# Routed attention and a gated feed-forward layer on one core: the first batch in query blocks of 128, 256 and 384, with the feed-forward layer's input and output halves as separate pieces

## The chip, the cores and the metric

The kernel runs on one core of a Trainium2 chip. The metric is the device time of one execution in microseconds (us); lower is better. Most executions of one kernel agree within 1%. A time without further words is a median; a "span" is the time from the first to the last instruction of the profiled execution, some 2 us less than the time.

Five engines work side by side, each with its own instruction queue: PE (TensorE matmuls; PEld is its weight load), ACT (ScalarE), DVE (VectorE), POOL (GpSimd) and SP (here it only issues DMAs).

## The reference, cut to what matters

```python
batch, n_heads, seq, head_dim = (4, 8, 768, 64)     # 16 clusters
q_assign = argmax(q_n . c_n)                        # nearest centroid, per head
k_assign = argmax(k_n . c_n)
mask = q_assign[:, :, :, None] == k_assign[:, :, None, :]
scores = where(mask, scale * q @ k.T, -1e9)
attn = softmax(scores)                              # the sum has + 1e-9 added
x = (attn @ v).transpose(0, 2, 1, 3).reshape(3072, 512)
gate = 1 / (1 + exp(-(x @ w_gate)))                 # 512 -> 1536
val = x @ w_val
return (gate * val) @ w_out                         # 1536 -> 512, float32
```

## The kernel before

For each batch, Q and K are turned so that the head dimension lies on the partitions (the tile `T`). Sixteen more rows hold the one-hot cluster of each query or key, scaled by 2048. A score matmul then contracts 80 rows, and a pair of the same cluster gets a large bonus, which is taken off again as the bias of the exp. That is the whole mask. To build the one-hot rows a batch needs a chain of steps: load, split into a high and a low half (DVE), transpose, logits against the centroids (PE, matmuls of 16 columns), one-hot (DVE), transpose of the one-hot, and a copy of its rows to partitions 64 to 79 of `T`.

A batch is worked off in two blocks of 384 queries. A block has 24 steps (4 pairs of heads times 6 chunks of 128 keys). A step is two score matmuls, one exp and six AV matmuls of 65 columns. The AV matmuls of a step stand one step behind its exp:

```python
    def att(b, qb):
        pend = None
        def av_part(pr, j, es, av):
            ...                                     # six matmuls of 65 columns
            if j == NCH - 1:                        # end of a pair of heads
                s = smp.tile([128, 2, QCH, D + 1], FP, name="avs")
                nc.vector.tensor_tensor(s, av, SV[b], ALU.add)   # operands cut
                ...                                 # 1/sum, then x on POOL
        for pr in range(NPR):
            for j in range(NCH):
                sc = scp.tile([128, 2, 512], FP, name="sc")
                for hh in range(2):
                    nc.tensor.matmul(out=sc[:, hh, 0:QB], ...)   # 80 rows, 384 columns
                es = esp.tile([128, 2, QB], HP, name="es")
                nc.scalar.activation(es, sc[:, :, 0:QB], AF.Exp, bias=nbias, scale=es_scale)
                yield
                if pend is not None:
                    av_part(*pend)
                if j == 0:
                    av = avp.tile([128, 512], FP, name="av")
                pend = (pr, j, es, av)
                yield
        av_part(*pend)
        ...                                         # xT: DMA transpose of x
```

The feed-forward layer (FFN) of a block is one generator of 132 matmuls (96 of 384 columns into `f`, with tanh on ACT, then 36 of 512 columns). It is fed in small portions between the attention steps of the next block. So the first block has no FFN to mix with, and the last block's FFN runs alone at the end.

The preparation of the next batch is laid out by a plan of steps. Its one-hot rows come last, for all heads at once, by a DMA transpose and then eight row DMAs for each side:

```python
    def prep_oh(b, side):
        ohf = OH[b, side].rearrange("p c h x -> p (c h x)")
        nc.vector.tensor_scalar(ohf, ohf, OHV, None, ALU.mult)
        ohT = ohp.tile([128, NCH, 128], HP, name=f"ohT{side}")
        nc.sync.dma_start_transpose(out=ohT, in_=ohf)
        for h in range(H):
            nc.sync.dma_start(out=T[b, side][D : D + NCL, h, :], in_=...)

    # in plan(b): steps of the 48 of the batch before
        if b == 1:
            a_at = (18, 24, 30, 35)                 # splits and DMA transposes, per pair
            b_at = (26, 32, 38, 42)                 # logits and one-hot, per pair
            oh_at = 44
        else:
            a_at, b_at, oh_at = (4, 12, 20, 27), (12, 20, 28, 35), 37
        ...
        at(oh_at, prep_oh, b, 1)
        at(oh_at + 1, prep_oh, b, 0)

    LAG = 5                                         # steps before the FFN of the block before starts
    for b in range(B):
        for qb in range(NQB):
            for half, _ in enumerate(att(b, qb)):
                if half == 2 * LAG and prev is not None:
                    fq.append(ffn(*prev))
                ...                                 # preparation of the plan
                ffn_some(132.0 / (2 * NST + 1))
```

Batch 0 prepares pair 0, and pair 1 but for its one-hot rows, before its first step, and the rest between the steps of its first block. Everything stands in program order on every engine (`tc.manual_schedule()`).

The softmax here doesn't subtract the row's maximum and nothing guards it: scores larger than these inputs give would overflow.

## Time and profile before

| | before |
|---|---|
| time, median of 3 runs (range) | 385.73 us (383.76 to 386.23) |
| span of the profiled run | 381.8 us |
| mean granted TensorE clock | 0.924 |
| first exp / last exp of batch 0 | 21.5 / 100.6 us |
| first FFN matmul | 66.6 us |
| first exp of batches 1, 2, 3 | 111.0, 195.8, 277.8 us |

The page of the profile gives each engine's busy time with its share of the span, and then 40 equal slices of the span (9.5 us each), each with a digit in tenths. PEclk is the clock that TensorE was granted.

```profile
PE 352.7 (92%) x3570; PEld 218.5 (57%) x3570; DVE 161.7 (42%) x319; ACT 234.5 (61%) x322; POOL 59.7 (16%) x62
...
PE   8777897999749979999999799999999999999995
...
PEclk9859655799959989999999989999999999999999
```

PE is the bound, but it is not evenly used: apart from the very last slice, and two slices (15 and 23) in which AV waits 2.3 us for DVE, the low digits of both rows lie in the first twelve slices. The next view sums each engine's busy time in chosen stretches; the columns are named in its first line.

```profile
core 0: us, PE busy (x) PEld busy (x) DVE busy (x) ACT busy (x) POOL busy (x), PEclk, DMA share, GB/s
22.00:40.00 18.00, 14.14 (x192) 10.85 (x193) 10.09 (x18) 9.57 (x11) 4.60 (x3) 0.85 1.15 212
40.00:58.00 18.00, 17.06 (x175) 9.15 (x172) 7.11 (x14) 13.96 (x15) 2.46 (x2) 0.53 0.76 212
58.00:73.00 15.00, 13.39 (x129) 8.03 (x128) 10.77 (x17) 7.54 (x10) 4.19 (x5) 0.54 0.92 177
73.00:100.00 27.00, 26.05 (x359) 18.20 (x357) 15.05 (x34) 17.89 (x27) 2.93 (x3) 1.00 0.38 84
100.00:120.00 20.00, 12.60 (x74) 5.75 (x73) 2.85 (x6) 5.77 (x8) 0.82 (x1) 0.74 0.43 105
```

Between 40 and 58 us PE is "busy" 17.06 of 18.00 us and yet does only 175 matmuls, at a clock of 0.53; between 73 and 100 us it does 359 in 27 us at full clock. Busy time alone hides this. The timeline of the same kernel (start, duration, engine, line, operation, and in brackets the idle time before it and what ended it) shows one step at the low clock:

```profile
52.71 0.83 PE L380 MATMUL sc<-T_184,T_185 80*128 80x384 f16 x2
...
53.45 0.35 PEld L343 LDWEIGHTS <-es 128*128 128x128 f16 x6 [0.60 <-ACT es L388]
53.45 0.51 PE L343 MATMUL av<-va,es 128*128 128x65 f16 x6
53.64 0.90 ACT L388 ACTIVATE es<-sc,nbias 128x768 f16<-128x768 f32 x1 [0.24 <-PE sc L380]
```

PE's weight load waits for the exp and the exp waits for the scores, so neither engine is full.

The chain of waits (the work that ended last, in order of time: start, duration, what) shows a second loss, at the start of batch 1:

```profile
102.12 0.45 PE f L434 x2
...
105.13 2.79 DMA ohT_1649<-oh_422
...
107.94 1.85 DMA T_421<-ohT_1649
...
109.92 0.48 PE sc L380
```

From 102.5 to 109.9 PE waits: first for the SP queue, then for the transpose of the one-hot tile, then for the row DMAs. The list of waits (engine and line, what it waited for, total us, times, longest) sizes that, and the stalls of AV behind the V-mean addition:

```profile
PE sc L380 <- DMA T_421<-ohT_1649: 7.4, 1, 7.4
...
PE av L343 <- DVE avs L353: 5.5, 3, 2.3
```

### The profile page before, as it was taken

Reading aid. Unit: us, or ns where it says so; the run is one execution under the profiler, and the core shown is the slowest. Engines: PE = TensorE matmul, PEld = TensorE weight load, DVE = VectorE, ACT = ScalarE, POOL = GpSimd, SP = SyncE. Lnnn points to the kernel's source line nnn. Section 1 sums busy time; section 2 is a strip of 40 time slices with the busy share of each in tenths; the row PEclk is TensorE's granted clock in tenths of the full one; section 3 lists DMA queues with packets and bytes.
Section 4 is the critical chain, followed back from the end, with each engine's and each line's share of the span. In section 5 each row is a group of like instructions: output and inputs, shape, how many; then the busy total and the mean of one; then the engine's idle time right before and its main releaser. Section 6 shows DMA issues by size and latency. Waiting matters only on the chain.

```text
span 381.8 us, 8564 instructions
## 1 busy us (share of the span) xinstructions
PE 352.7 (92%) x3570; PEld 218.5 (57%) x3570; DVE 161.7 (42%) x319; ACT 234.5 (61%) x322; POOL 59.7 (16%) x62
## 2 busy tenths in 40 slices
PE   8777897999749979999999799999999999999995
PEld 3655644667415646566656566566656655665552
DVE  5765628475303456635315637534303421331330
ACT  3347676566416747576767565676768877884331
POOL 5943103200100000320000000220000010100000
PEclk9859655799959989999999989999999999999999
DMA  7999788940129682780239674941230004002202
GB/s 246 297 215 209 220 195 134 277 98 10 39 54 267 183 198 72 127 228 19 45 73 267 167 219 85 193 102 30 49 103 29 0 3 124 1 2 47 79 2 82
DMA packets 76071, 45.72 MB, mean 120 GB/s; under 512 B 57152, under 2 KB 71936, under 8 KB 76032
## 3 DMA queue, kind: packets, MB, share of 16 engines
q1 hardware_dynamic: 73280, 40.42, 42.6%
q0 software_dynamic: 2608, 4.72, 6.7%
q8 instruction: 28, 0.46, 0.5%
q14 instruction: 11, 0.09, 0.1%
q10 hardware_dynamic: 144, 0.03, 0.0%
HBM read 28.34 MB, written 6.29 MB: 91 GB/s over the span
## 4 chain that ended last, share of the span: by engine, by line
PE 80%; DMA 5%; issue 4%; POOL 3%; DVE 3%; ACT 2%; SPq 1%; ACTq 0%; POOLq 0%; DVEq 0%
PE f L416 33%; PE f L434 17%; PE sc L380 16%; PE av L343 9%; PE f L186 3%; DMA nat<-in_q_dram 2%; POOL hl L173 2%; DMA xT<-x 2%; PE f L317 1%; ACT es L388 1%; DVE hl L174 1%; DMA ohT_1649<-oh_422 1%; SPq L76 1%; DVE avs L353 1%; DVE hl L173 1%
## 5 line engine op out<-in xcount | busy, mean ns | idle before, releaser
L388 ACT ACTIVATE es<-sc,nbias 128x768 f16<-128x768 f32 x192 | 172.6, 901 | 92.5 <-PE sc L380 89.5
L427 DVE SCALAR_TENSOR_TENSOR hT<-g,f 128x384 f16<-128x384 f32 x96 | 53.0, 553 | 119.8 <-PE f L416 81.8
L416 PE MATMUL f<-xT,wg 128*128 128x384 f16 x384 | 99.0, 333 | 1.2 <-DMA xT<-x 1.2
L416 PE MATMUL f<-xT,wv 128*128 128x384 f16 x384 | 93.2, 329 | 0.5 <-ACT g L425 0.5
L343 PEld LDWEIGHTS <-es 128*128 128x128 f16 x1152 | 63.0, 102 | 43.2 <-issue 9.4
L434 PE MATMUL f<-wo,hT 128*128 128x512 f16 x288 | 78.0, 388 | 0.0
L343 PE MATMUL av<-va,es 128*128 128x65 f16 x1152 | 70.9, 200 | 6.7 <-DVE avs L353 5.5
L365 POOL TENSOR_TENSOR x<-avs,ri 128x384 f16<-128x384 f32 x32 | 27.9, 873 | 285.6 <-DVE ri L364 214.1
L425 ACT ACTIVATE g<-f 128x384 f32<-128x384 f32 x96 | 46.8, 487 | 23.5 <-PE f L416 13.8
L416 PEld LDWEIGHTS <-wg 128*128 128x128 f16 x384 | 34.5, 99 | 19.5 <-issue 3.6
L416 PEld LDWEIGHTS <-wv 128*128 128x128 f16 x384 | 33.5, 98 | 16.3 <-issue 1.5
L434 PEld LDWEIGHTS <-hT 128*128 128x128 f16 x288 | 25.7, 99 | 21.6 <-issue 2.3
L174 DVE SCALAR_TENSOR_TENSOR hl<-nat,hl 128x768 f16<-128x768 f32 x32 | 33.5, 1046 | 3.0 <-POOL hl L173 2.1
L380 PE MATMUL sc<-T_184,T_185 80*128 80x384 f16 x96 | 31.4, 420 | 0.5
L380 PE MATMUL sc<-T_421,T_423 80*128 80x384 f16 x96 | 24.7, 337 | 7.4 <-DMA T_421<-ohT_1649 7.4
L173 DVE TENSOR_SCALAR hl<-nat 128x768 f16<-128x768 f32 x26 | 18.1, 696 | 22.1 <-DMA nat<-in_k_dram 22.0
L353 DVE TENSOR_TENSOR avs<-av,sv 128x390 f32<-128x390 f32 x32 | 17.9, 559 | 20.6 <-PE av L343 20.5
L380 PE MATMUL sc<-T_1731,T_1733 80*128 80x384 f16 x96 | 23.9, 330 | 0.0
L197 DVE TENSOR_REDUCE mx<-f 128x12 f32<-128x192 f32 x32 | 11.3, 354 | 28.9 <-PE f L186 28.9
L380 PE MATMUL sc<-T_3046,T_3048 80*128 80x384 f16 x96 | 23.5, 325 | 0.0
L443 ACT ACTIVATE osb<-f 128x512 f32<-128x512 f32 x24 | 14.3, 594 | 13.5 <-PE f L434 12.9
L380 PEld LDWEIGHTS <-T_423 80*128 80x128 f16 x96 | 9.6, 101 | 15.9 <-issue 9.1
(82 smaller groups left out, 199.7 us busy)
## 6 DMA issues: line engine op xcount, KB each, us to landing
nat<-in_k_dram SPq DMA_DIRECT2D x16, 384.0 KB, 5.4
nat<-in_q_dram SPq DMA_DIRECT2D x16, 384.0 KB, 6.0
vn<-in_v_dram SPq DMA_DIRECT2D x8, 768.0 KB, 5.6
out_dram<-osb SPq DMA_DIRECT2D x24, 256.0 KB, 2.7
wg<-in_moe_w_gate_dram POOLq DMA_DIRECT2D x1, 1536.0 KB, 12.3
wv<-in_moe_w_val_dram POOLq DMA_DIRECT2D x1, 1536.0 KB, 19.7
wo<-in_moe_w_out_dram POOLq DMA_DIRECT2D x1, 1536.0 KB, 27.0
T_423<-ohT_1618 SPq DMA_DIRECT2D x8, 24.0 KB, 1.9
```

Source lines behind the costliest of these rows:

```text
L173: (eng or nc.vector).tensor_scalar(hl[:, :, 0, :], nat, SC, None, ALU.mult)
L174: nc.vector.scalar_tensor_tensor(hl[:, :, 1, :], nat, SC, hl[:, :, 0, :], ALU.mult, ALU.subtract)
L343: nc.tensor.matmul(out=av[:, o : o + D + 1], lhsT=es[:, hh, bass.ts(t, 128)], rhs=VA[b][:, 2 * pr + hh, j, :], start=(j == 0 and hh == 0 a ...
L353: nc.vector.tensor_tensor(s, av[:, 0 : 2 * QCH * (D + 1)].rearrange("p (h t d) -> p h t d", h=2, t=QCH), SV[b][:, 2 * pr : 2 * pr + 2, :] ...
L365: nc.gpsimd.tensor_tensor(x[:, :, 2 * pr * D : 2 * (pr + 1) * D].rearrange("p t (h d) -> p h t d", h=2), s[:, :, :, 0:D], ri.unsqueeze(3). ...
L380: nc.tensor.matmul(out=sc[:, hh, 0:QB], lhsT=T[b, 1][0 : D + NCL, h, bass.ts(j, 128)], rhs=T[b, 0][0 : D + NCL, h, bass.ts(qb, QB)], start ...
L388: nc.scalar.activation(es, sc[:, :, 0:QB], AF.Exp, bias=nbias, scale=es_scale)
L416: nc.tensor.matmul(out=gv[i][:, 0:QB], lhsT=w[:, dc, bass.ts(fc, 128)], rhs=xT[:, :, dc, :], start=(dc == 0), stop=(dc == NDC - 1),)
L425: nc.scalar.activation(g, gv[0][:, 0:QB], AF.Tanh, scale=0.5)
L427: nc.vector.scalar_tensor_tensor(hT[:, fc, :], g, 1.0, gv[1][:, 0:QB], ALU.add, ALU.mult)
L434: nc.tensor.matmul(out=o, lhsT=hT[:, fc, bass.ts(t, 128)], rhs=wo[:, fc, :], start=(fc == 0), stop=(fc == NFC - 1),)
L443: nc.scalar.activation(osb, o, AF.Copy, scale=0.5)
```

## The change

The intent is to start sooner and to have FFN work to mix in sooner:

- **Batch 0 in three blocks.** The first has 128 queries. It needs every key of the batch but only a sixth of the queries (`qn0`, loaded first), and has eight exps, each over three key chunks. The second has 256 queries and takes the first one's FFN input half. The third has 384 queries and takes the first one's output half and the whole FFN of the second.
- **FFN as two generators**, `ffn_in` and `ffn_out`; the first block's output half is held back (`held`) to the third block. The weights come in ten pieces instead of three.
- **AV stands two steps behind the exp** in blocks of 256 and 384 queries.
- **One-hot rows per pair of heads**, turned by PE transposes (`rows`), in place of one DMA transpose for all heads; the splits of a pair are issued half a step apart.
- **V sums on POOL** (`sum_v`), so in batches 1 to 3 a mean takes one matmul where six stood.
- **Order by a model.** In the first block and up to the middle of the third, the compiler's scheduler is free to reorder PE, ACT and DVE by its own model of times. It keeps program order only on SP and POOL.
- **Smaller parts.** In batch 0, half of each split of K runs on ACT where most stood on POOL (2.17 us each). The first two pairs of batch 1, and `x` of the first two blocks, are transposed by PE. In the kernel before, a DMA transposed `x`, and its first transpose took 6.14 us, up to the first FFN matmul. In batches 1 to 3 the FFN starts 7 steps into a block instead of 5.

The core of the diff, with cuts marked by "...":

```diff
-    ctx.enter_context(tc.manual_schedule())
+    first = ExitStack()
+    first.enter_context(tc.manual_schedule())
...
-    load_pair(0, 0)
-    load_pair(0, 1)
+    qn0 = natp.tile([128, H, D], FP, name="nat")
+    nc.sync.dma_start(out=qn0, in_=...)             # 128 queries of every head
+    for pr in range(NPR):
+        load_side(0, pr, 1)                         # all keys
     load_v(0, 0)
-    load_pair(0, 2)
-    load_pair(0, 3)
     load_v(0, 1)
+    for pr in range(NPR):
+        load_side(0, pr, 0)                         # queries last
...
-    def prep_oh(b, side):
-        ...                                         # DMA transpose, 8 row DMAs
+    def rows(b, pr):
+        ns = 1 if b == 0 else 2
+        po = fp_.tile([32 * ns, 1024], HP, name="f")
+        for c in range(NCH):
+            nc.tensor.transpose(po[:, bass.ts(c, 128)], ..., ident)
+        ohc = ohp.tile([32 * ns, S], HP, name="ohc")
+        nc.vector.tensor_scalar(ohc, po[:, 0:S], OHV, None, ALU.mult)
+        for side in range(ns - 1, -1, -1):
+            for hh in range(2):
+                nc.sync.dma_start(out=T[b, pr, side][D : D + NCL, hh, :], in_=...)
...
+    def sum_v(b, g):
+        ...                                         # three additions on POOL
...
-    def att(b, qb):
+    def att(b, c0, n):
+        pend = []
+        G = 3 if n == 1 else 1                      # key chunks per exp
...
-                if pend is not None:
-                    av_part(*pend)
+                if len(pend) == (1 if G > 1 else 2):
+                    av_part(*pend.pop(0))
+                pend.append((pr, j0, es))
...
-    def ffn(b, qb):
+    def ffn_in(b, c0, n):
+    ...
+    def ffn_out(b, c0, n):
...
+    BLK = [[(0, 1), (1, 2), (3, 3)]] + [[(0, 3), (3, 3)]] * (B - 1)
...
+    def by_dma(b, pr, load, a, base):
+        at(base, load, load_pair, b, pr)
+        for i, side in enumerate((1, 0)):
+            at(base, a + 0.5 * i, split, b, pr, side)
+            at(base, a + 0.5 * i, trans_dma, b, pr, side)
+            at(base, a + 9 + i, classify, b, pr, side)
+        at(base, a + 11.5, rows, b, pr)
...
+    def first_block():
+        ...
+        first.close()
+        first.enter_context(
+            tc.manual_schedule(engines={mybir.EngineType.SP, mybir.EngineType.Pool})
+        )
+        ...
+            if pr == 2:
+                prep_v(0, 3, nc.scalar)             # the V cast of the last pair, on ACT
...
+                lag = 14 if b > 0 else {1: 7, 3: 9}[c0]
+                pieces = {(0, 1): 110, (0, 3): 132}.get((b, c0), 132)
+                for half, _ in enumerate(att(b, c0, n)):
+                    if (b, c0, half) == (0, 3, 24):
+                        first.close()
+                        ctx.enter_context(tc.manual_schedule())
+                    if half == lag:
+                        fq.append(ffn_in(*prev))
+                        if (b, c0) == (0, 1):
+                            held.append(ffn_out(*prev))
+                        else:
+                            fq += held
+                            held = []
+                            fq.append(ffn_out(*prev))
```

## The prediction

> **What bounds the kernel now.** TensorE, once fed. The busy table gives PE 352.7 of 381.8 us. In the timeline from 123 us, one attention step (two score, six AV, 5.5 FFN matmuls) takes 1.4 to 1.5 us without a gap: 0.33 + 0.18 + 5.5 x 0.1625. A full-clock block of 384 queries with an FFN block is then about 35.5 us of PE, the whole kernel about 323 (estimate: 8 blocks, 32 logit groups at 0.75, V sums, batch-0 transposes). The other 59 us are lost, about 44 of them before 110 us:
> - The first exp starts at 21.5 us (timeline).
> - From 38 to 73 us the granted clock is 0.5 to 0.57 (windows): block 0 has no FFN, ACT and PE wait for each other, the first FFN matmul waits for xT until 66.6. The Trainium skill, "TensorE: Matmul & The Clock Gate", Part 1, says half rate is the default and returns after an idle window; this trace agrees (0.50 in 50 to 60 us).
> - From 102.5 to 109.9 PE waits for batch 1's one-hot rows (chain of waits: issue queue, DMA transpose, row DMAs), then runs at half clock to about 116.
> - At 134.2 and about 216 AV waits 2.3 us for the V-mean addition, which stands behind two splits in VectorE's queue.
>
> **What the change does.**
> 1. Block of 128 queries first: first exp at about 13.5 us, 8 earlier. Eight exps (0.90) suffice, but it carries all K preparation, 20 to 23 us each of ACT and DVE work: it ends at 33 to 38.
> 2. 256 queries with FFN input for the first 128: PE about 18.5 us at full clock, ACT about 20; ends at 54 to 60. FFN starts near 38, not 66.6.
> 3. 384 queries with 96 FFN-in matmuls of 256 columns (0.108), 36 FFN-out (0.216) and batch 1's preparation: about 40 us of PE; batch 1 starts at 95 to 98, not 110.
> 4. Batch 1's rows come per pair: the 7.4 us stall goes (part of the 95), plus about 3 us at half clock.
> 5. Later batches: AV lags two steps and splits are issued apart, so the 2.3 us stalls and clock dips mostly go (3 to 5). V sums lose 10 of 12 matmuls of 0.115 per batch (3.4).
> 6. Added on PE: transposes for two pairs of batch 1 (3.4), row transposes (4.7 over three batches, 2.6 more in batch 0), short FFN matmuls (1.2): about 12 us.
>
> **Sum.** Batch 1 starts 13 us earlier (steps 1 to 4 less their added work), 3 of clock, 7 from step 5, minus 3 of row transposes after batch 0: 20 us. Span about 360, time **363 us**, range **354 to 375**. Chances: faster 0.87, same 0.09, slower 0.04.
>
> **What would show it.** First exp before 15 us; first FFN matmul before 42; first scores of batch 1 before 100 with no wait over 2 us on row DMAs; clock above 0.8 on average in 40 to 100; batches 2 and 3 about 80 us apart, not 82; the tail (last FFN block) unchanged.
>
> **What would make it wrong.** The 128-query block is a long chain over four in-order engines: if it ends after 42, the gain halves. The clock may stay at half in the 256-query block. Weights load in ten pieces behind V: a late quarter stalls FFN. The first stage is ordered by a scheduler's model, perhaps badly.

## The result, and the profile after

| | before | after |
|---|---|---|
| time, median (range) | 385.06 us (383.76 to 386.23, 4 runs) | 365.42 us (364.88 to 366.35) |
| span | 381.8 | 363.4 |
| mean granted clock | 0.924 | 0.993 |
| first / last exp of batch 0 | 21.5 / 100.6 | 17.2 / 89.4 |
| first FFN matmul | 66.6 | 37.5 |
| first exp of batch 1 | 111.0 | 92.5 |
| first exp of batch 2 | 195.8 | 173.4 |
| first exp of batch 3 | 277.8 | 255.7 |
| from batch 1's first exp to the end | 270.8 | 270.9 |

The ratio is 0.949, with a 95% interval of 0.945 to 0.953. Executions over 1.5% slower than the fastest of the same kernel are left out of the means. (A ratio is the mean time of one kernel's runs over the mean of the other's runs of the same rounds, so it is not quite the ratio of the medians that are quoted. Below, the same pair of kernels gave 0.956, so a difference of 0.007, some 2.6 us, can be scatter.) The prediction of 363 (354 to 375) held. The last row of the table says that it held for reasons that have to be sorted out: the whole gain lies before batch 1.

The page after:

```profile
PE 344.6 (95%) x3887; PEld 228.1 (63%) x3887; DVE 169.5 (47%) x374; ACT 244.6 (67%) x359; POOL 71.5 (20%) x105
...
PE   8699999999989999989999999989999999999995
...
PEclk9989999999999999999999999999999999999999
```

PE does 317 more matmuls than before in 8.1 us less busy time, and the span is 18.4 us shorter. The Trainium skill, "Trainium Kernel Development and Optimization", Performance Expectations, says that the busy time of matmuls is a bad metric for how near a kernel is to its roofline (the least time that the hardware allows), because matmuls are pipelined. This agrees: PE's busy share only rose from 92% to 95%, and less than half of the gain in span appears as lower busy time.

The same stretches as before:

```profile
22.00:40.00 18.00, 16.57 (x314) 14.25 (x312) 15.54 (x44) 13.33 (x20) 0.00 (x0) 1.00 1.01 160
40.00:58.00 18.00, 16.58 (x265) 13.97 (x265) 12.55 (x33) 15.07 (x32) 3.29 (x4) 1.00 0.67 191
58.00:73.00 15.00, 14.97 (x258) 12.24 (x256) 10.15 (x27) 11.07 (x16) 4.87 (x8) 1.00 0.62 129
73.00:100.00 27.00, 26.08 (x314) 18.17 (x313) 12.83 (x29) 19.11 (x28) 9.78 (x12) 1.00 0.64 131
100.00:120.00 20.00, 18.72 (x226) 12.51 (x224) 10.41 (x21) 14.76 (x21) 1.80 (x2) 1.00 0.62 158
```

From 40 to 73 us the clock is 1.00 instead of 0.53 and 0.54, and PE issues 523 matmuls instead of 304.

The waits that answer to those shown before:

```profile
PE f L403 <- DVE ohc L284: 1.7, 2, 1.0
...
PE f L278 <- ACT g L540: 1.5, 2, 0.8
...
PE av L450 <- DVE avs L460: 0.7, 3, 0.4
```

The wait for the one-hot rows of batch 1 has left the list. The AV stall shrank from 5.5 to 0.7 us. New small waits stand at the V mean (L403) and at the row transposes (L278).

One place went differently from the prediction in the first 20 us. This is ACT's timeline:

```profile
9.18 0.86 ACT L193 ACTIVATE hl<-nat 128x768 f16<-128x768 f32 x1
13.24 0.83 ACT L368 CAST va<-vn 128x768 f16<-128x768 f32 x1 [3.20 <-DMA vn<-in_v_dram]
13.97 0.79 ACT L226 COPY T_291<-f 128x768 f16<-128x768 f16 x1
...
17.23 1.69 ACT L499 ACTIVATE es<-sc,nbias 128x768 f16<-128x768 f32 x2
```

In the program the cast of V for the last pair (L368) stands behind the fifth of the eight exps. The scheduler's model moved it ahead of the first exp, when its load had not landed. ACT waited 3.20 us with everything else behind it. The Trainium skill, "TensorE: Matmul & The Clock Gate", Part 1, on engine queue depths, says that ACT and DVE are strict first-in-first-out. This trace agrees: the copy behind the cast starts only when the cast is all but done, at 13.97 us (the cast runs from 13.24 us for 0.83 us; in the experiment without it, below, the copy starts at 12.46 us), and the first exp starts at 17.2 us, where 13.5 had been predicted.

The whole later part, from batch 1's first exp on, by batch:

```profile
92.50:173.40 80.90, 77.57 (x885) 49.91 (x884) 38.97 (x79) 55.65 (x78) 17.11 (x23) 1.00 0.54 134
173.40:255.70 82.30, 79.57 (x872) 50.27 (x869) 39.24 (x78) 55.87 (x78) 17.05 (x23) 1.00 0.54 131
255.70:363.40 107.70, 103.74 (x848) 60.87 (x843) 28.26 (x59) 65.03 (x96) 7.43 (x9) 0.99 0.14 42
```

These sum to 270.9 us, of which PE is busy 260.88 and idle 10.0. The kernel before took 270.8 for it (PE busy 261.82, idle 9.0), with the same 672 FFN input matmuls left in both (the output matmuls left are 277 to 281). This is where the predicted 7 us are missing.

### The profile page after: what moved, and what is told of

Same layout as the page of the kernel before. It is cut to its first block, busy times and chain, and to the rows that moved or that the text cites. A ratio compares the mean times of both kernels' runs of the same rounds, so it can differ in the third digit from the quotient of the medians.

```text
span 363.4 us, 9364 instructions
## 1 busy us (share of the span) xinstructions
PE 344.6 (95%) x3887; PEld 228.1 (63%) x3887; DVE 169.5 (47%) x374; ACT 244.6 (67%) x359; POOL 71.5 (20%) x105
## 4 chain that ended last, share of the span: by engine, by line
PE 78%; DMA 6%; DVE 5%; issue 5%; ACT 4%; SPq 1%; POOL 0%; ACTq 0%; DVEq 0%
PE f L531 30%; PE f L552 16%; PE sc L490 15%; PE av L450 8%; PE f L243 4%; DMA vn<-in_v_dram 3%; ACT es L499 2%; PE f L216 2%; DVE hl L195 1%; DMA out_dram<-osb 1%; PE f L278 1%; DVE hT L542 1%; DMA nat<-in_q_dram 1%; DMA nat<-in_k_dram 1%; PE f L295 1%
## 5 line engine op out<-in xcount | busy, mean ns | idle before, releaser
L499 ACT ACTIVATE es<-sc,nbias 128x768 f16<-128x768 f32 (+1 forms) x200 | 173.6, 877 | 71.1 <-PE sc L490 66.2
L542 DVE SCALAR_TENSOR_TENSOR hT<-g,f 128x384 f16<-128x384 f32 (+1 forms) x96 | 51.1, 534 | 84.0 <-PE f L531 46.4
L450 PEld LDWEIGHTS <-es 128*128 128x128 f16 x1152 | 59.8, 97 | 27.1 <-issue 3.7
L470 POOL TENSOR_TENSOR x<-avs,ri 128x384 f16<-128x384 f32 (+1 forms) x32 | 26.8, 837 | 245.5 <-DVE ri L469 196.6
L450 PE MATMUL av<-va,es 128*128 128x65 f16 x1152 | 67.5, 194 | 1.3 <-DVE avs L460 0.7
L540 ACT ACTIVATE g<-f 128x384 f32<-128x384 f32 (+2 forms) x108 | 48.8, 452 | 18.6 <-PE f L531 9.7
L552 PE MATMUL f<-wo_194,hT 128*128 128x512 f16 x138 | 38.3, 379 | 0.0
L552 PE MATMUL f<-wo_193,hT 128*128 128x512 f16 x138 | 38.1, 379 | 0.0
L460 DVE TENSOR_TENSOR avs<-av,sv 128x390 f32<-128x390 f32 (+2 forms) x36 | 18.6, 516 | 41.0 <-PE av L450 40.4
L531 PE MATMUL f<-xT,w_186 128*128 128x384 f16 (+2 forms) x108 | 25.6, 308 | 0.0
L531 PE MATMUL f<-xT,w_187 128*128 128x384 f16 (+2 forms) x108 | 25.6, 307 | 0.0
L531 PE MATMUL f<-xT,w_188 128*128 128x384 f16 (+2 forms) x108 | 24.1, 307 | 0.4 <-DVE hT L542 0.4
L531 PE MATMUL f<-xT,w_191 128*128 128x384 f16 (+2 forms) x108 | 24.0, 307 | 0.5 <-ACT g L540 0.5
L531 PE MATMUL f<-xT,w_189 128*128 128x384 f16 (+2 forms) x108 | 23.8, 307 | 0.5 <-DVE hT L542 0.5
L531 PE MATMUL f<-xT,w_192 128*128 128x384 f16 (+2 forms) x108 | 23.6, 307 | 0.4 <-DVE hT L542 0.4
L531 PE MATMUL f<-xT,w_190 128*128 128x384 f16 (+2 forms) x108 | 23.8, 307 | 0.0
L531 PE MATMUL f<-xT,w_185 128*128 128x384 f16 (+2 forms) x108 | 23.6, 308 | 0.2
L370 POOL CAST va<-vn 128x768 f16<-128x768 f32 x15 | 14.2, 951 | 10.6 <-DMA vn<-in_v_dram 10.6
## 6 DMA issues: line engine op xcount, KB each, us to landing
wo_193<-in_moe_w_out_dram POOLq DMA_DIRECT2D x1, 768.0 KB, 17.1
```

The lines of the kernel that those rows point to most:

```text
L370: nc.gpsimd.tensor_copy(va[:, :, :, 0:D], src)
L450: nc.tensor.matmul(out=av[:, o : o + D + 1], lhsT=es[:, hh, bass.ts(g * n + t, 128)], rhs=VA[b, pr][:, hh, j0 + g, :], start=(j0 + g == 0 ...
L460: nc.vector.tensor_tensor(s[:, :, 0:n, :], av[:, 0 : 2 * n * (D + 1)].rearrange("p (h t d) -> p h t d", h=2, t=n), SV[b][:, 2 * pr : 2 * p ...
L470: (nc.vector if n == 1 else nc.gpsimd).tensor_tensor(x[:, 0:n, 2 * pr * D : 2 * (pr + 1) * D].rearrange("p t (h d) -> p h t d", h=2), s[:, ...
L499: nc.scalar.activation(es[:, :, 0:w], sc[:, :, 0:w], AF.Exp, bias=nbias, scale=es_scale)
L531: nc.tensor.matmul(out=gv[i][:, 0:w], lhsT=wgv[i][fc * NQ // NFC][:, dc, bass.ts(fc % (NFC // NQ), 128)], rhs=xT[:, 0:n, dc, :], start=(dc ...
```

## The experiments

The theory was this. (1) The gain comes from batch 0: the small first block lets FFN work begin early, which fills PE and keeps its clock up, and batch 1's preparation no longer stalls. (2) The lag and the V sums do save time in later batches, but new work on PE takes it back. The rivals were that the gain comes from something that the title does not list (batch 1's earlier preparation alone, or the scheduler's order), that the half clock by itself was the loss, and that the lag is worth nothing.

The runs came in three calls. Each call has its own chip or rounds, and its own runs of the kernel before (medians of the fast ones 382.61, 382.55 and 383.50 us). Ratios compare better than times do.

| run | built on | time, median (range), us | ratio to before [95%] |
|---|---|---|---|
| a0_after | after | 365.27 (364.84–368.34) | 0.956 [0.951, 0.961] |
| x2_ffnlate | after | 373.37 (371.49–374.26) | 0.974 [0.968, 0.979] |
| x4_vcast | after | 363.45 (363.03–363.89) | 0.949 [0.945, 0.954] |
| x7_manual | after | 378.83 (375.84–381.26) | 0.989 [0.984, 0.995] |
| x1_b1early | before | 374.01 (372.76–375.22) | 0.978 [0.973, 0.983] |
| x9_warm | before | 374.56 (372.93–376.74) | 0.980 [0.974, 0.986] |
| x3_avlag1 | after | 376.58 (374.01–378.32) | 0.983 [0.974, 0.991] |
| x8_splits | after | 366.15 (366.11–366.49) | 0.958 [0.951, 0.965] |
| x11_lag2 | before | 371.75 (370.57–372.13) | 0.969 [0.966, 0.973] |
| x12_model | before | 377.27 (375.47–378.34) | 0.984 [0.980, 0.988] |
| x5_mean | after | 368.94 (368.42–372.98) | 0.965 [0.960, 0.970] |
| x13_vcast_rowsdma | after | 367.65 (366.25–369.16) | 0.959 [0.956, 0.963] |

All twelve gave correct results. The stages, read as starts of exps in the timelines of the profiled runs (us):

| run | first exp | last exp of batch 0 | first exp of batch 1 | from there to the end | span |
|---|---|---|---|---|---|
| before | 21.5 | 100.6 | 111.0 | 270.8 | 381.8 |
| after | 17.2 | 89.4 | 92.5 | 270.9 | 363.4 |
| a0_after | 17.7 | 90.8 | 94.0 | 272.5 | 366.5 |
| x2_ffnlate | 17.5 | 98.2 | 101.0 | 270.7 | 371.7 |
| x4_vcast | 15.7 | 87.7 | 90.8 | 270.6 | 361.4 |
| x7_manual | 15.5 | 102.3 | 105.5 | 271.7 | 377.2 |
| x1_b1early | 22.5 | 98.2 | 103.9 | 269.5 | 373.4 |
| x9_warm | 22.5 | 101.0 | 106.0 | 268.9 | 374.9 |
| x3_avlag1 | 17.7 | 100.3 | 103.7 | 272.8 | 376.5 |
| x8_splits | 17.1 | 90.5 | 93.6 | 270.7 | 364.3 |
| x11_lag2 | 23.2 | 98.4 | 104.2 | 264.8 | 369.0 |
| x12_model | 20.7 | 104.9 | 110.8 | 264.8 | 375.6 |
| x5_mean | 17.4 | 91.1 | 94.3 | 276.8 | 371.1 |
| x13_vcast_rowsdma | 15.1 | 88.3 | 90.9 | 274.2 | 365.1 |

### The change again, beside the others: a0_after

No edit.

> The changed kernel itself, so that variants of it can be compared with it on the same chip: 364.9 to 366.4 us as in its own four runs. No theory expects anything else.

Its runs fall into two groups, 364.8 to 365.4 and 368.1 to 368.3 us. The profiled run, 368.34, is one of the upper group. So a difference of 3 us between two profiled runs of this family can be the kernel's own scatter.

### FFN input of the first block moved to the third block: x2_ffnlate

```diff
-                pieces = {(0, 1): 110, (0, 3): 132}.get((b, c0), 132)
+                pieces = {(0, 1): 110, (0, 3): 228}.get((b, c0), 132)
...
-                        fq.append(ffn_in(*prev))
                         if (b, c0) == (0, 1):
-                            held.append(ffn_out(*prev))
+                            held += [ffn_in(*prev), ffn_out(*prev)]
                         else:
                             fq += held
                             held = []
+                            fq.append(ffn_in(*prev))
                             fq.append(ffn_out(*prev))
```

> The FFN input half of the first 128 queries is moved from the 256-query block to the 384-query block (same work, 96 matmuls of 128 columns). Theory A (the prediction's step 2: early FFN work fills TensorE while ScalarE sets the pace of the 256-query block, and keeps the clock up): the 256-query block gets only a little shorter, TensorE's granted clock in it falls below 0.9, the 384-query block gets 6 to 7 us longer, and the time rises by 3 to 6 us. Rival B (TensorE is the limit in both blocks, so the work is only moved): the time stays within 1 us of the changed kernel.

It takes 373.37 us, 8.1 more than the change beside it. The 256-query block is as long as in a0_after without the FFN work as with it. The first line is x2_ffnlate, the second a0_after, each over its own 256-query block (stretch, length, PE, PEld, DVE, ACT, POOL, clock):

```profile
35.20:57.80 22.60, 19.36 (x272) 15.48 (x271) 13.37 (x32) 16.88 (x26) 3.58 (x4) 0.81 0.56 139
```

```profile
35.50:58.30 22.80, 21.14 (x358) 17.63 (x357) 15.80 (x44) 18.33 (x38) 3.29 (x4) 1.00 0.50 144
```

So 86 more matmuls cost 0.2 us there: without them PE is less filled and the clock is 0.81. The same FFN work in the 384-query block, which is full already, lengthens it from 32.5 (58.3 to 90.8) to 40.4 us (57.8 to 98.2): PE is busy 37.69 us of it instead of 31.55 and idle 2.71 instead of 0.95, at a clock of 0.94 instead of 1.00. Rival B is refuted, and the loss is larger than the 3 to 6 us of theory A. This is the core of the change: here FFN work was almost free where attention alone did not fill PE, and cost about 8 us in the full block. One reservation holds for every variant of batch 0 of the changed kernel: the scheduler orders these blocks by its model, and with another program it may choose another order, so that an edit's effect and the new order's cannot be told apart.

### The V cast of the last pair on POOL: x4_vcast

```diff
-                prep_v(0, 3, nc.scalar)
+                prep_v(0, 3)
```

> The one V cast that the changed kernel gives to ScalarE goes to GpSimd, like the other three. In the changed kernel the scheduler put it in ScalarE's queue at 13.2 us, where it waits 3.2 us for V from memory with everything behind it held up, the first exp among it. Theory A (this wait is on the chain that starts attention): first exp at about 14 us instead of 17.2, batch 1 starts 2 to 3 us earlier, time lower by 2 to 3 us. Rival B (VectorE and the other preparation set the pace of the 128-query block anyway): the first exp is earlier but the block ends at the same time, and the time changes by less than 1 us.

363.45 us, 1.8 less by the medians, and every one of its runs (363.03 to 363.89) is below every run of a0_after (from 364.84). ACT's timeline:

```profile
12.46 0.80 ACT L226 COPY T<-f 128x768 f16<-128x768 f16 x1 [3.05 <-PE f L216]
...
15.72 1.69 ACT L499 ACTIVATE es<-sc,nbias 128x768 f16<-128x768 f32 x2
```

The first exp comes at 15.7 us instead of 17.2. The wait did not vanish: ACT now waits 3.05 us for PE's transposes, which the cast's wait had covered. Of 4.0 us (3.20 of waiting and 0.83 of the cast) only about 1.5 were to be had at the first exp. The rest of the kernel is unchanged (270.6 us from batch 1 on), so the gain arrives at the end whole. So theory A holds in kind; the first exp comes later than its 14 us, and the gain is a little under its 2 to 3 us. This is the fastest version measured, faster than both kernels.

### Program order throughout: x7_manual

```diff
-        first.close()
-        first.enter_context(
-            tc.manual_schedule(engines={mybir.EngineType.SP, mybir.EngineType.Pool})
-        )
...
-                    if (b, c0, half) == (0, 3, 24):
-                        first.close()
-                        ctx.enter_context(tc.manual_schedule())
```

(The manual schedule is entered once, for the whole kernel.)

> The changed kernel with all engines in the written order throughout; in the changed kernel TensorE, VectorE and ScalarE are ordered by the scheduler's model from the first attention block to the middle of the third. Theory A (the model's order hides latencies of a long chain over four engines): the 128-query block ends later than 33 us and batch 1 starts 3 to 8 us later than 91.9 us, with nothing changed after it. Rival B (the written order is as good, and it avoids the 3.2 us wait of the V cast): the same time within 1 us, or 2 us less.

378.83 us: 13.6 us slower than the change, and only 1.1% faster than the kernel before. Batch 1 starts 11.5 us later than in a0_after (theory A: 3 to 8), and the part from there on is as long (271.7 against 272.5). Its first exp is earlier (15.5 us: no cast ahead of it), but the 128-query block then takes from 15.5 to 37.4 us for its exps, where the change takes from 17.2 to 31.3. The stretch from 15 to 33 us, x7_manual first, then the change:

```profile
15.00:33.00 18.00, 15.00 (x220) 14.30 (x221) 8.89 (x23) 11.90 (x15) 6.22 (x9) 0.63 1.29 216
```

```profile
15.00:33.00 18.00, 16.19 (x302) 14.75 (x299) 15.22 (x40) 15.74 (x20) 5.76 (x9) 0.91 1.29 215
```

In program order DVE does 23 instructions there where the model's order does 40, and PE runs at 0.63 of its clock. The prediction had named the model's order as a risk; it is a large part of the gain. With all its parts but this one, in the order in which it is written, the change brings 1.1%. That order was not tuned for program order.

### Batch 1's preparation four steps earlier, in the kernel before: x1_b1early

```diff
-            a_at = (18, 24, 30, 35)
-            b_at = (26, 32, 38, 42)
-            oh_at = 44
+            a_at = (14, 20, 26, 31)
+            b_at = (22, 28, 34, 38)
+            oh_at = 40
```

> The kernel before, with batch 1's preparation started four steps earlier in batch 0's plan and nothing else changed, so that the one-hot rows can land before batch 0's attention ends. Theory A (the 7.4 us stall at 102.5 us is only a matter of the plan, and the half clock after it follows from the stall): the stall goes, batch 1 starts 7 to 10 us earlier and the time falls to 375 to 378 us; then the block structure of the change is worth only the remaining 10 to 12 us. Rival B (the rows are late because the queue that issues them or the loads are the limit): the stall stays above 3 us and the time above 381 us.

374.01 us, a gain of 8.5 us from nine numbers in a plan. The wait for the rows, which was 7.4 us, is now (95 to 112 us):

```profile
PE sc L380 <- DMA T<-ohT: 2.6, 1, 2.6
```

So close to half of the change's gain can be had in the kernel before without any new block. The prediction's figure for this was 7.4 and about 3 of half clock behind it; the measured 8.5 is between the 7.4 and their sum.

### Idle matmuls in the steps of the first block, with that plan: x9_warm

Built on x1_b1early. After each step of the first block and after the first six steps of the second:

```diff
+                if b == 0 and half % 2 == 1 and (qb == 0 or half < 2 * LAG + 2):
+                    t = fp_.tile([128, 512], FP, name="f")
+                    for _ in range(2):
+                        nc.tensor.matmul(
+                            out=t, lhsT=wz[:, 0:128], rhs=wz, start=True, stop=True
+                        )
```

> As the run with batch 1 planned earlier, and with two idle matmuls of 512 columns after each attention step that has no FFN work beside it in batch 0 (60 in all, 13 us of TensorE at full clock), to keep TensorE's clock up. Theory A (the half clock from 38 to 73 us itself costs time, as score and AV matmuls at half rate and ScalarE wait for each other): the granted clock there rises above 0.85, block 0 ends 3 to 6 us earlier and the time falls by that much below the run without idle matmuls. Rival B (the half clock is only a sign of idle time, the pace is set by ScalarE and by preparation): the clock rises but the time changes by less than 1.5 us, or grows by the added work.

374.56 us, the same as x1_b1early. The clock did come up; this is the stretch that had 0.53 in the kernel before and in x1_b1early:

```profile
40.00:58.00 18.00, 16.60 (x228) 10.19 (x229) 11.66 (x21) 13.42 (x15) 2.67 (x2) 1.00 0.87 218
```

The block's last exp came at 58.7 us, against 57.7 without. Sixty idle matmuls of 512 columns take 13 us of PE at 0.216 each. As an estimate from the durations at full clock, a step with them needs 0.33 + 0.18 + 0.43 = 0.94 us of PE; without them, at half clock, it needs twice 0.33 + 0.18, or 1.02 us. The traces fit: in this stretch exps follow each other every 1.08 us with idle matmuls and every 1.12 us in x1_b1early. So, by this estimate, the idle matmuls cost about what the clock bought, and the run cannot say what the half clock costs by itself. It does show that two more matmuls per step took the granted clock from 0.53 to 1.00, and that the full clock alone brought no time here. One idle matmul per step was not tried.

### AV one step behind again, in the changed kernel: x3_avlag1

```diff
-                if len(pend) == (1 if G > 1 else 2):
+                if len(pend) == 1:
```

> The changed kernel with AV one step behind the scores in all blocks, as before the change, instead of two. Theory A (step 5 of the prediction: the longer lag takes away waits of TensorE for VectorE and ScalarE in the later batches): the time rises by 3 to 5 us, with waits of AV for the V-mean addition of about 2 us each again. Rival B (the lag does not matter once the splits are spread): within 1 us of the changed kernel.

376.58 us, 11.3 more than the change. But the loss is not where the lag had been expected to act. The later batches differ by 0.3 us (272.8 against a0_after's 272.5; the first profile of the changed kernel has 270.9), and the wait of AV for the V-mean addition comes back with only 0.8 us twice, not with 2 us each. In these batches, which are in program order and have the splits set apart, the lag is thus worth little: neither theory holds as it was written. In batch 0 the 256-query block takes 29.6 us instead of 22.8 and the 384-query block 35.3 instead of 32.5:

```profile
35.40:65.00 29.60, 23.98 (x356) 19.34 (x355) 15.90 (x44) 18.96 (x39) 3.51 (x5) 0.88 0.60 149
```

PE is busy 23.98 of 29.60 us there. The run has a flaw: in batch 0 the scheduler orders by its model, and with another program it chose another order. It is not shown that the lag alone makes the 11 us. For the lag by itself a kernel in program order was needed:

### AV two steps behind, in the kernel before: x11_lag2

Built on x1_b1early, which is in program order throughout.

```diff
-                if pend is not None:
-                    av_part(*pend)
-                if j == 0:
-                    av = avp.tile([128, 512], FP, name="av")
-                pend = (pr, j, es, av)
+                if len(pend) == 2:
+                    av_part(*pend.pop(0))
+                pend.append((pr, j, es))
                 yield
-        av_part(*pend)
+        for p in pend:
+            av_part(*p)
```

> The kernel before with two parts of the change and without its blocks: batch 1 planned four steps earlier (374.0 us alone) and AV two steps behind the scores instead of one. Theory A (what shortened batch 0 is that TensorE no longer waits for the exp of the step just before; the blocks of 128 and 256 queries are a smaller part): block 0, 35 to 36 us from first to last exp with lag 1, shortens to 27 to 31 us and the time falls to 365 to 369 us. Rival B (the early small block and the early FFN work are the gain, the lag only matters inside them): block 0 stays above 33 us and the time above 372 us.

371.75 us, ratio 0.969 against 0.978: a gain of 0.85%, 3.3 us (the intervals just touch, so 1 to 6 us is possible). Theory A fails: batch 0 hardly moves (its first block's exps take 33.8 us instead of 35.2; PE waits there once 2.5 us for row DMAs that the lag cannot hide). The gain is in the later batches:

```profile
104.20:185.30 81.10, 79.56 (x854) 50.09 (x853) 38.79 (x76) 55.77 (x79) 9.55 (x10) 0.98 0.57 139
185.30:264.90 79.60, 78.06 (x853) 49.61 (x852) 38.81 (x77) 55.61 (x78) 10.37 (x11) 1.00 0.63 140
264.90:369.00 104.10, 100.12 (x805) 58.84 (x803) 25.40 (x53) 64.66 (x96) 7.42 (x9) 1.00 0.14 43
```

These sum to 264.8 us, against 269.5 in x1_b1early. The wait of AV for the V-mean addition, 4.5 us in x1_b1early from batch 1 on, has left the list; FFN matmuls that wait 2.6 us for DVE have come in its place. PE is idle for 2.1 us less (7.05 instead of 9.13) and busy for 2.6 us less, at a mean clock of 1.00 instead of 0.98. So the mechanism of step 5 is real here, where the splits stand together. It is worth 4.7 us by these two profiles; x1_b1early's is the slowest of its runs, so that 3.3 us is the better figure. And this kernel's later batches are 6.1 us shorter than the changed kernel's 270.9, although both have the lag. That is no accident of one profile: x12_model has 264.8 too, and a0_after, x2_ffnlate, x4_vcast and x8_splits have 270.6 to 272.5. So the changed kernel gives it back: over the stretch it has PE busy 260.88 against 257.75 us, 3.1 more, and idle 10.0 against 7.05 us, 3.0 more. The busy part has names in the trace: 54 transposes of one-hot rows, 4.65 us, and 48 logit matmuls of batch 1's last pair, which now come after its first exp, 1.5 us. The V sums that went are to be taken off: 5 matmuls stand where 24 stood, some 2.2 us (an estimate from 0.69 us for six of them in the kernel before).

### The scheduler's order in the kernel before: x12_model

Built on x11_lag2: the same switch as in the change, just before the main loop, and back at the middle of the second block.

```diff
+    first.close()
+    first.enter_context(
+        tc.manual_schedule(engines={mybir.EngineType.SP, mybir.EngineType.Pool})
+    )
...
+                if (b, qb, half) == (0, 1, 24):
+                    first.close()
+                    ctx.enter_context(tc.manual_schedule())
```

> As the run before it, and TensorE, VectorE and ScalarE ordered by the scheduler's model from the first attention block to the middle of the second, as the change does. The written order in the changed kernel cost 13.5 us. Theory A (the model's order is worth as much here, where preparation of three pairs also runs beside attention): block 0 shortens by 3 to 8 us more, time 358 to 364 us, below the changed kernel. Rival B (the order matters only for the chain of small pieces in the 128-query block): within 1.5 us of the run without it.

377.27 us, 5.5 slower than x11_lag2 beside it: neither a gain as in the change nor no effect. The later batches are equal (264.8 both); batch 0's first block now ends at 64.2 instead of 57.0 us. DVE's timeline:

```profile
29.32 0.94 DVE L175 SCALAR_TENSOR_TENSOR hl<-nat,hl 128x768 f16<-128x768 f32 x1
35.79 0.56 DVE L174 TENSOR_SCALAR hl<-nat 128x768 f16<-128x768 f32 x1 [5.53 <-DMA nat<-in_k_dram]
```

The model put a split of batch 1 at the head of DVE's queue before its load had landed, and everything of batch 0 behind it waited 5.53 us. It is the error of the V cast again, larger. Whether it makes the whole of the 7.2 us by which the block ends later was not looked into. The model's order is worth 13.6 us in one program and costs 5.5 in the other, so "let the scheduler order it" is no rule.

### The two splits of a pair at the same step: x8_splits

```diff
-            at(base, a + 0.5 * i, split, b, pr, side)
-            at(base, a + 0.5 * i, trans_dma, b, pr, side)
+            at(base, a, split, b, pr, side)
+            at(base, a, trans_dma, b, pr, side)
```

> The changed kernel with the two splits of a pair issued in the same half step, as before the change, instead of half a step apart. Theory A (the spacing takes the VectorE queue out of TensorE's way): the time rises by 1 to 3 us, with longer waits of FFN matmuls and AV for VectorE. Rival B (the half step is too small to matter): within 0.7 us.

366.15 us; 0.7 to 0.9 us more than the change by ratio and by median, with an interval (0.951 to 0.965) that holds the change's own 0.956. From batch 1 on it took 270.7 us, like the change, although FFN matmuls wait 3.1 us for DVE there (0.9 in the change). With the lag at two steps, setting the splits apart is worth nothing that could be told from the scatter. Inconclusive, and small in any case.

### V means by matmuls again: x5_mean

```diff
-        if b == 0:
-            for c in range(NCH):
-                ...
-        else:
-            nc.tensor.matmul(out=sp[:, 0:n], lhsT=ones, rhs=VS[b][...], ...)
+        for i in range(len(hs) // 2):
+            w = 2 * (D + 1)
+            for c in range(NCH):
+                ...                                 # out=sp[:, i * w : (i + 1) * w]
...
-        at(b - 1, e + 34, sum_v, b, 0)
-        at(b - 1, e + 44, sum_v, b, 1)
```

> The changed kernel with the V sums of batches 1 to 3 made by TensorE again (24 matmuls of 130 columns a batch, about 0.065 us each at full clock) instead of additions on GpSimd and two matmuls. Theory A (the prediction's step 5): TensorE is the limit there, so the time rises by 3 to 4 us. Rival B (GpSimd's and VectorE's waits bind as well): less than 1.5 us.

368.94 us, ratio 0.965 against 0.956: 3.4 us, on two chips, with intervals that touch (0.960 to 0.970 and 0.951 to 0.961), so that anything from 0.5 to 6 us is possible. It is the size that the prediction gave to the V sums (3.4). The profiled run shows more, 276.8 us from batch 1 on, but it is the slowest of its runs (372.98). It stands in for 24 short matmuls where the kernel before had 12 wide ones, so it is not exactly the old form.

### One-hot rows by DMA for two pairs at once: x13_vcast_rowsdma

Built on x4_vcast, the fastest version. For batches 2 and 3 and the last two pairs of batch 1, the one-hots of two pairs go into one tile, one DMA transpose turns it, and eight row DMAs spread it:

```diff
+    def rows2(b, g):
+        ohf = OH2[b, g].rearrange("p c u s h x -> p (c u s h x)")
+        nc.vector.tensor_scalar(ohf, ohf, OHV, None, ALU.mult)
+        ohT = ohp.tile([128, NCH, 128], HP, name="ohT", bufs=1)
+        nc.sync.dma_start_transpose(out=ohT, in_=ohf)
+        ...                                         # 8 row DMAs
...
-        at(base, a + 11.5, rows, b, pr)
+        if pr % 2 == 1:
+            at(base, a + 11.5, rows2, b, pr // 2)
```

> A version meant to beat both kernels: the V cast on GpSimd (363.5 us alone), and the one-hot rows of two pairs at a time turned by one DMA transpose instead of 12 matmuls, for batches 2 and 3 and half of batch 1 (60 matmuls of 0.083 us less, 10 VectorE evictions of 0.55 us less). Theory A (step 6 of the prediction: the row transposes are on the critical engine): 4 to 5 us less than with the V cast alone, 358.5 to 360 us. Rival B (the DMA queue now delays rows, loads or xT): waits for rows or xT over 1 us, and a gain below 2 us.

367.65 us, ratio 0.959 against x4_vcast's 0.949: about 4 us slower, although PE's busy time fell from 343.2 to 340.6 us. The PE work saved came back as waits, in part on the SP queue. First the SP queue's timeline, then the list of waits from batch 1 on:

```profile
179.69 6.12 SPq L309 DMA_DIRECT2D T<-ohT  x8
185.90 3.19 SPq L584 DMA_DIRECT2D out_dram<-osb  x3
```

```profile
ACT osb L583 <- DMA out_dram<-osb: 4.7, 2, 3.7
PE f L553 <- ACT osb L583: 4.3, 2, 3.7
```

Eight row DMAs hold the queue for 6.12 us. Three stores of output tiles stand behind them. ACT waits 3.7 us for the buffer of one of these stores (until 188.1 us), and PE waits 3.7 us for ACT. In all, the waits of PE in the list from batch 1 on are 12.7 us, against 5.3 in x4_vcast. This chain makes 4.3 of them; the others are mainly for DVE (5.5) and for ACT's tanh (2.0), and where they come from was not traced. So 4.65 us of PE transposes are the cheaper of the two forms tried here, and the 6.1 us between the changed kernel and x11_lag2 in the later batches are not won back this way. The old form, one transpose for all heads of a side, was not put into the changed kernel.

## Why the prediction was right or wrong

The total was right: 363 predicted, 365.42 measured. Two of its terms were off by 5.5 and 7.1 us in opposite directions, and they cancelled: that the total came within 2.4 us was luck. By the stages of the profile:

| | predicted | measured |
|---|---|---|
| batch 1 starts earlier by | 13 us | 18.5 us |
| from there to the end, saved | 7 us (3 clock + 7 of step 5 − 3 row transposes) | −0.1 us |
| sum | 20 us | 18.4 us |

1. **Step 1, the first block.** Predicted: first exp at about 13.5 us, block end at 33 to 38. Measured: 17.2 us; the block's last exp starts at 31.3 and the next block's first at 34.2. The first figure was 3.7 us too early. ACT's queue held a cast that waited 3.20 us for its load, and x4_vcast shows that this cost 1.5 us; without it ACT waits 3.05 us for PE's transposes there, and the other 2.2 us of the miss were not taken apart. The block's end was right.
2. **Step 2, FFN in the second block.** Predicted: FFN near 38, block end at 54 to 60, and the clock might stay at half. Measured: first FFN matmul at 37.5, next block's first exp at 56.9, clock 1.00. x2_ffnlate puts 8.1 us on this term (with the reservation about the order), and shows why: the FFN matmuls fit into the block without lengthening it.
3. **Step 3, the third block.** Predicted: about 40 us of PE, batch 1's first scores at 95 to 98. Measured: from 56.9 to 92.5, 35.6 us, of which PE is busy 34.66; first score at 91.9. The term was sized too long by about 5 us of PE. This is one of the two mis-sized terms, and it made the prediction of batch 1's start too pessimistic.
4. **Step 4, batch 1's rows.** Predicted: the 7.4 us stall goes, and about 3 us of half clock. Measured: the wait is gone and the clock is 1.00 from 100 to 120 us. x1_b1early shows 8.5 us for the same aim by a plan alone. So a gain of this size was to be had from the plan's timing, without the blocks.
5. **Step 5, the later batches.** This is the step whose sum failed: "AV lags two steps and splits are issued apart, so the 2.3 us stalls and clock dips mostly go (3 to 5)", V sums 3.4, and "3 of row transposes after batch 0" set against them, so a net saving. The mechanisms hold: x11_lag2 saves 4.7 us from batch 1 on (3.3 of the whole time by the ratios), and x5_mean's ratio gives 3.4 us for the V sums. But x11_lag2 has its splits together. In the changed kernel either the lag or the spacing of the splits can be taken out with little loss in these batches (x3_avlag1: 272.8, x8_splits: 270.7), so one of the two seems to be enough there; no run takes out both. But the net is nil. Against x11_lag2 the changed kernel has 3.1 us more of PE work (row transposes 4.65 us rather than 3, and 1.5 us of logits that slid behind batch 1's start) and 3.0 us more of PE idle time, which no term of the prediction held. The two waits that are new in the list after, at the V mean (1.7 us) and at the row transposes (1.5 us), are of that size together. But x11_lag2 has waits of its own: the lists from batch 1 on sum to 5.6 us in the change and to 3.1 in x11_lag2. So that these two waits are the whole of it is argued and not shown. "Batches 2 and 3 about 80 us apart" was wrong: 82.3, as before (82.0); in x11_lag2 they are 79.6 apart.
6. **The tail** was predicted unchanged, and it is: 15.60 us for 96 input matmuls and 7.78 us for 36 output matmuls in both.
7. **The model's order.** The prediction called it a risk. x7_manual shows that it is worth 13.6 us against the order as written, the largest single effect measured; x12_model shows that it is not good by itself.

As a sum, from ratio to ratio: the kernel before to x1_b1early, 8.5 us; to x11_lag2, 3.3 more; to the change, about 5 more (0.969 against 0.956), of which the V sums are 3.4. (By their intervals the 5 us can be 3 to 8.) Those 5 us are a net. At batch 1's first exp the change is 11.7 us ahead of x11_lag2 (92.5 against 104.2): that is what the blocks, the early FFN, the model's order and the smaller parts bring together. From there to the end it then gives 6.1 us back (270.9 against 264.8). Within the changed kernel the parts hang together: without the early FFN it loses 8.1 us, without the model's order 13.6.

What stays open: what the blocks are worth in an order that is as good and not the model's; what the half clock costs by itself; how much of x3_avlag1's loss is the lag and how much the new order; what the smaller parts bring, of which the transposes of `x` by PE and the splits on ACT change just the start of the kernel; and whether the changed batch 0 with the old preparation of the later batches would keep both gains (as an estimate from the stage table, 90.8 us of x4_vcast and 264.8 us of x11_lag2 make 355.6 us of span, if nothing that crosses the border between the two parts costs extra). That kernel was not built.

## What to carry to other kernels

Look for the stretch where the bounding engine is not filled by the work at hand, and move independent work there; here 86 matmuls more cost 0.2 us in such a stretch, and moving them to a full one cost about 8 us. Check at which stage a gain arrives and whether the later stages keep it: equal time from batch 1 on showed at once that two gains had been paid back, by new work on the same engine and by new waits. Before a restructuring, try the plan's numbers alone: moving one preparation four steps earlier brought 8.5 of the 18 us or so.

## What the Trainium skill lacked or had wrong

- "TensorE: Matmul & The Clock Gate", "Why this matters for your kernels", advises to leave no idle gap of over about 3 us between bursts of matmuls. That is not enough here. In the kernel before, the granted clock fell to half at about 41.0 us and stayed there until about 71.7 us. The last gap of PE before the fall was 2.40 us long (36.76 to 39.16), the longest within the stretch 1.19 us; between 40 and 58 us PE was busy 17.06 of 18.00 us by the profile. Idle matmuls in the same steps brought the clock from 0.53 to 1.00. (The prediction cites Part 1 of the page for the half rate and its return after an idle window. This trace agrees with the half rate, 0.50 from 50 to 60 us, but shows no gap there that could have been the window.) Another section of the page does name many small idles between groups of matmuls, for a case of cycling PSUM buffers; the advice itself leaves that out.
- The same page, Part 2, "Back-to-back issue gap", gives about 131 ns for a matmul of 512 columns in a sustained stream with its weight loads. Here 36 such matmuls with their weight loads took 7.78 us, 216 ns each, and 96 of 384 columns took 15.60 us, 162.5 ns each, at full clock in both kernels. That is the page's figure for the single gap (Part 1: 215.7 ns), not its sustained one.
- No page was found that tells what an order chosen by a scheduler's model does in strict queues when the model does not know when a load lands. Here it parked a waiting instruction at the head of a queue twice (3.20 us on ACT, 5.53 us on DVE), and the same switch was worth 13.6 us in one program and cost 5.5 us in another.
- No page was found that says how a burst of small DMA issues delays a store on the same queue and through it the compute engines ("Perfetto Trace Analysis", DMA Optimizations, where it would belong, only advises to balance issues over engines and to keep inputs and outputs apart): eight row DMAs held the SP queue for 6.12 us, and ACT then waited 3.7 us and PE 3.7 us for the buffer of a store behind them.
